# A convolution with a soft mixture of experts: two pieces of x in one DMA issue, with the loads of taps and w1 between the issues

## The chip, the cores and the metric

The kernel runs on one core of a Trainium2 chip. The metric is the device time of one execution in microseconds (us). The engines are named as in the profile: PE (TensorE, the matmuls; PEld its weight loads), DVE (VectorE), ACT (ScalarE), POOL (GpSimd) and SP (SyncE), which computes nothing here and issues all DMAs.

## The reference

There are two steps. The first is a causal convolution along the sequence with seven taps, where the taps of each token and head are the softmax of `weight_gen`. The second is a soft mixture of experts over the 28,672 rows that come out of it: each of 32 slots takes a softmax-weighted mean of all rows, eight experts work on four slots each, and each row takes a softmax-weighted mean of the 32 slots' outputs.

```python
# x: (8, 3584, 192); weight_gen: (8, 3584, 8 heads, 7 taps)
w = np.exp(weight_gen - weight_gen.max(-1, keepdims=True))
w = w / (w.sum(-1, keepdims=True) + 1e-09)
x_unf = x_pad[:, idx, :].reshape(B, S, K, H, group)      # six rows of zeros ahead of x
x = np.einsum('bshk,bskhg->bshg', w, x_unf).reshape(B * S, D)

logits = x @ phi                                          # (28672, 32)
d = np.exp(logits - logits.max(0)); d /= d.sum(0) + 1e-09 # over the rows
slot_input = (d.T @ x).reshape(E, S_per_e, D)
for e in range(E):
    slot_out[e] = np.maximum(slot_input[e] @ w1[e], 0.0) @ w2[e]
c = np.exp(logits - logits.max(1, keepdims=True)); c /= c.sum(1, keepdims=True) + 1e-09
out = c @ slot_out.reshape(n_slots, D)
```

All data are float32.

## The kernel before

The sequence is cut into 1,104 short stretches of 26 tokens each. Four stretches make a group (276 groups), two groups a pair (138 pairs), and four pairs a block (35 blocks, counted by `k`). x comes in pieces: a piece `t` holds four groups, that is two pairs, so there are 69 pieces and block k reads the pieces 2k and 2k+1. The taps come in chunks of eight groups, one chunk per block.

**Convolution as matmuls.** For each group the seven taps of each token are laid out as a band matrix of 32 x 26, and PE multiplies bands with x (`conv`, L230, 32 matmuls per pair). For this x lies block-diagonally in `big`: a piece fills four fields `h = 0..3`, each on its own 32 partitions and with its own DMA (`loadx`, L156), and the rest of the field was zeroed once at the start. `big` has room for five pieces (`NXS`); `place(t)` says where piece t goes, which is t modulo 5, except that piece 0 goes where piece 4 goes. So a piece can be loaded when the piece that had its place before has been read by PE.

**From taps to bands.** A chunk's taps are loaded (`loadw`, L160, three buffers) and then pass through a chain: `tap_top` on DVE (maximum, L171), `tap_sub` on POOL (L175), `tap_exp` on ACT (L179), `tap_sum` on POOL (L188 to L190), `tap_inv` on DVE (reciprocal, L194), `tap_mul` on POOL (L202, into `wide`), `tap_turn` on DVE (L206, from `wide` into one of three bands).

**The rest of a block.** ACT copies the convolved rows out of PSUM (L236). PE turns them (`pt`, L250), and ACT copies that to `cm` (L257). The pairs are handled further in units of eight pairs, two blocks: PE forms the unit's logits (`ls`, L281), DVE their maximum (`mx`, L288; `mq`, L290), PE spreads it over the partitions (`newmax`, L306), DVE takes the result (`nm`, L310), ACT the exponential (`dd`, L318), DVE turns it (`dt`, L327), and PE adds up slot inputs (`acb`, L346), which DVE gathers in `accS` (L354). From block 2 on, in even blocks `ls` of the unit before stands between the second and third pair, and newmax behind the fourth; in odd blocks acb stands between the third and fourth pair.

**What sets the order.** The operations are recorded by `op(engine, cost, reads, writes, function, ..., late=..., due=...)`, with an estimated cost and, for a DMA, `late`, the time that is allowed from its issue to its landing. A planner, `model`, goes through the list four times. PE's and SP's operations keep the order in which they are recorded; those of DVE, ACT and POOL are placed where the planner finds that they can start, those with the least time to spare first. So another cost or `late` of a DMA, or another order of SP's operations, gives DVE, ACT and POOL another order too. Each engine then works through its list in order: an instruction that waits holds up all behind it.

The loads of a block are recorded behind its conv: the taps of chunk k+4, then the pieces 2k+5 and 2k+6 as their places come free, with a part of w1 (24 parts in all) behind some pieces.

After the last pair, the experts' matmuls (`hidden`, `outputs`) and the output rows (`rows`, L818, and `leave`, L825 and L827) follow.

Of the kernel before, what the change touches and what calls it, by code (L numbers as in the profile page):

```python
# [20 lines left out]
SGG = 4  # L21
UP = 8
NSG = NG // SGG
NBC = SGG * 4 * 2
L = 32
CH = 2
NCH = -(-NG // (4 * CH))
# [3 lines left out]
NS, E, SE, F = 32, 8, 4, 1024  # L31
# [5 lines left out]
Q = 4  # L37
TR = 3 * 32 + T
NXS = 5
# [6 lines left out]
def place(t):  # L46
    return t % NXS if t else NXS - 1
# [3 lines left out]
def conv_soft_moe(ctx, tc, xh, wh, phi, w1a, w1b, w2, out):  # L51
# [101 lines left out]
    def loadx(t):  # L153

        for h in range(4):
            SY.dma_start(xbd[32 * h : 32 * h + 32, place(t), h], xh[t, h])  # L156

    def loadw(c):
        n = min(CH, NG // 4 - CH * c)
        SY.dma_start(taps[c % NTAP][:, 0:n], wh[c, :, 0:n])  # L160

    ALL = slice(0, CH)
    tops, tsums = {}, {}

    def each(t, n):
# [249 lines left out]
        SY.dma_start(w2_at(e, 0, FC), w2[:, e])  # L415

    def pace(e, what, src):
        op(PO, 0.15, [what], [("w2", e), x_of(NSG - NXS + e // 2)], mark, e, src)
        op(SP, 0.4, [("w2", e)], [], loadw2, e)

    logit, dispatched = {}, {}
# [7 lines left out]
    def op(eng, cost, reads, writes, f, *a, late=0.0, due=None):  # L429


        i = len(ops)
        preds = {writer[r] for r in (*reads, *writes) if r in writer}
        for r in writes:
            preds |= set(readers.get(r, ()))
            writer[r], readers[r] = i, []
        for r in reads:
            readers.setdefault(r, []).append(i)
        preds.discard(i)
        ops.append((eng, cost, late + 0.1 * (eng == "TE"), preds, due, f, a))  # L440

    def x_of(t):
        return ("x", place(t))

    def conv_reads(p):
        return {x_of(g // SGG) for g in (2 * p, 2 * p + 1)} | {("band", p // 4 % NBAND, p // 2 % CH)}

    def tm_of(p):
        u, pr = unit(p)
# [2 lines left out]
    VE, AC, PO, TE, SP = "VE", "AC", "PO", "TE", "SP"  # L452
    op(SP, 0.65, [], [("w", 0, 0), ("w", 0, 1)], loadw, 0, late=2.6)
    op(SP, 0.65, [], [("w", 1, 0), ("w", 1, 1)], loadw, 1, late=2.6)
    op(SP, 2.6, [], [x_of(0)], loadx, 0, late=2.8)
    op(SP, 0.6, [], [("w", 2, 0), ("w", 2, 1)], loadw, 2, late=3.0)
    op(SP, 1.9, [], [x_of(1)], loadx, 1, late=3.0)
    for t, es in ((2, (PO, AC, AC, AC)), (3, (PO, AC, VE, AC)), (NXS, (PO, PO, AC, AC))):
        for h, e in enumerate(es):
            op(e, 0.77, [], [("z", t, h)], clear, place(t), h, {PO: G, AC: A, VE: V}[e])  # L460
        if t < NXS:
            op(SP, 1.9, [("z", t, h) for h in range(4)], [x_of(t)], loadx, t, late=3.0)
    for i in range(NCV):
        op(AC, 0.47, [], [("cv", i)], clear_cv, i)
    op(VE, 0.3, [], [("tm", u, pr) for u in range(NTM) for pr in range(UP)], edges)
# [79 lines left out]
    for k in range(BLOCKS):  # L545
# [8 lines left out]
        for c in range(3, NCH):  # L554
            if k == max(0, c - 2):
                chain(c)
        for c in range(NTAP, NCH):
            if k == max(0, c - 4):
                op(SP, 0.4, [], [("w", c % NTAP, b) for b in range(CH)], loadw, c, late=4.0)
        for t in range(NSG):  # L560
            if (SGG * t + SGG - 1) // (2 * Q) == k:
                if t + NXS < NSG:
                    for i in (NXS - 1, NXS) if t == 0 else (t + NXS,):
                        op(SP, 2.0, [("z", i, h) for h in range(4)], [x_of(i)], loadx, i, late=3.0)
                    if t == 0:
                        op(SP, 0.45, [], ["phi"], SY.dma_start, phi_sb, phi, late=3.0)
                for j in range(2 * (E + E // 2)):
                    if 2 + 5 * j // 2 == t:
                        e, f = j // 2, slice(F // 2 * (j % 2), F // 2 * (j % 2 + 1))
                        to, w, e = (w1a_sb, w1a, e) if e < E else (w1b_sb, w1b, e - E)  # L570
                        op(SP, 0.4, [], [], SY.dma_start, to[:, e, f], w[:, e, f])
        for p in ps:
            e = p - (PAIRS - 9)
            if e >= 0 and e % 2 == 0:
# [357 lines left out]
```

## Time and profile before

| | us |
|---|---|
| median of three runs | 309.73 (305.82 to 310.65) |
| the profiled execution's own time | 308.94 |
| span in the profile | 307.2 |
| PE busy | 265.4 (86%) |
| DVE busy | 197.8 (64%) |
| ACT busy | 190.3 (62%) |
| POOL busy | 146.5 (48%) |
| convolution's first and last matmul | 8.2 and 222.4 |
| x: issues, one's landing (median) | 276, 3.2 |
| taps: issues, one's landing (median) | 35, 3.7 |
| mean granted clock of PE | 0.945 of full speed |

The profiled execution's own time is 1.74 us longer than its span, which runs from the first to the last instruction. A row of a timeline gives the start and the duration in us, the engine and the line, the operation, what it writes and reads, how many instructions are merged in it, and in brackets the engine's idle time before it with what ended it. Issues on SP's queue are the time in which SP hands a DMA over, not that in which it moves. A row of waits gives the total, the number of times and the longest.

### The profile page before, as it was taken

Reading aid. Unit: us, or ns where it says so; the run is one execution under the profiler, and the core shown is the slowest. Engines: PE = TensorE matmul, PEld = TensorE weight load, DVE = VectorE, ACT = ScalarE, POOL = GpSimd, SP = SyncE. Lnnn points to the kernel's source line nnn. Section 1 sums busy time; section 2 is a strip of 40 time slices with the busy share of each in tenths; the row PEclk is TensorE's granted clock in tenths of the full one; section 3 lists DMA queues with packets and bytes.
Section 4 is the critical chain, followed back from the end, with each engine's and each line's share of the span. In section 5 each row is a group of like instructions: output and inputs, shape, how many; then the busy total and the mean of one; then the engine's idle time right before and its main releaser. Section 6 shows DMA issues by size and latency. Waiting matters only on the chain.

```text
span 307.2 us, 15262 instructions
## 1 busy us (share of the span) xinstructions
PE 265.4 (86%) x6646; PEld 213.6 (70%) x6646; DVE 197.8 (64%) x337; ACT 190.3 (62%) x399; POOL 146.5 (48%) x254
## 2 busy tenths in 40 slices
PE   8898996999998999899899989999999888899100
PEld 8887975889887988789788878898768622233000
DVE  8867738775975957868478568573158489994100
ACT  9886673767685778667566666675422188786300
POOL 8856456654568194774654553520027345540000
PEclk9999998999999999999999999999999999879555
DMA  6758666867675767767567667657647079999994
GB/s 184 217 171 236 201 199 195 208 178 207 197 211 150 225 188 207 207 192 212 168 183 212 189 185 211 189 156 227 217 121 296 2 303 403 399 398 398 399 399 177
DMA packets 30161, 69.24 MB, mean 225 GB/s; under 512 B 6288, under 2 KB 11152, under 8 KB 30096
## 3 DMA queue, kind: packets, MB, share of 16 engines
q1 hardware_dynamic: 30096, 68.28, 69.2%
q8 instruction: 52, 0.85, 1.1%
q14 instruction: 13, 0.11, 0.1%
HBM read 46.21 MB, written 22.04 MB: 222 GB/s over the span
## 4 chain that ended last, share of the span: by engine, by line
PE 73%; DVE 6%; DMA 6%; issue 5%; ACT 2%; POOL 2%; DVEq 0%; POOLq 0%; ACTq 0%
PE cv L230 31%; PE pt L250 15%; PE ls L281 8%; PE acb L346 8%; PE po L818 5%; DMA out<-big 4%; PE so L763 2%; PE hpb L742 2%; PE acb L306 2%; DMA taps<-wh 2%; DVE big L825 1%; ACT big L825 1%; DVE band L206 1%; DVE big L362 1%; DVE cT L404 1%
## 5 line engine op out<-in xcount | busy, mean ns | idle before, releaser
L230 PE MATMUL cv<-big,band 128*26 128x96 f32 x4416 | 112.0, 250 | 4.0 <-issue 2.6
L230 PEld LDWEIGHTS cv<-big,band 128*26 128x26 f32 x4416 | 100.8, 130 | 13.8 <-issue 8.1
L236 ACT COPY tm<-cv 128x384 f32<-128x384 f32 x138 | 66.5, 484 | 62.8 <-PE cv L230 62.5
L206 DVE STREAM_TRANSPOSE band<-wide 128x1664 f32<-128x1664 f32 (+1 forms) x37 | 65.4, 1771 | 6.1 <-POOL wide L202 6.0
L250 PE MATMUL pt<-ident,tm 122*128 122x122 f32 x414 | 51.0, 273 | 0.0
L257 ACT COPY cm<-pt 128x416 f32<-128x416 f32 x103 | 48.1, 512 | 1.7 <-PE pt L250 0.6
L250 PEld LDWEIGHTS pt<-ident,tm 122*128 122x128 f32 x414 | 44.7, 145 | 2.3
L202 POOL TENSOR_TENSOR wide<-exps,sum 128x364 f32<-128x364 f32 (+1 forms) x36 | 28.4, 791 | 24.9 <-DVE sum L194 18.6
L818 PE MATMUL po<-cT,so 32*128 32x442 f32 (+3 forms) x256 | 35.4, 644 | 5.6 <-DVE big L825 3.0
L175 POOL TENSOR_TENSOR taps<-taps,top 128x364 f32<-128x364 f32 (+1 forms) x36 | 28.5, 793 | 18.3 <-DVE top L171 17.9
L825 ACT COPY big<-po 128x884 f32<-128x884 f32 (+2 forms) x33 | 28.5, 894 | 9.3 <-PE po L818 5.3
L188 POOL TENSOR_TENSOR si<-exps 128x208 f32<-128x208 f32 x32 | 20.2, 632 | 28.4 <-ACT exps L179 28.0
L818 PEld LDWEIGHTS po<-cT,so 32*128 32x128 f32 (+1 forms) x256 | 12.3, 172 | 27.5 <-ACT big L825 15.7
L281 PE MATMUL ls<-cm,phi_sb 128*32 128x208 f32 x544 | 29.1, 338 | 2.0 <-issue 1.9
L346 PE MATMUL acb<-tm,dt 128*32 128x193 f32 x544 | 27.4, 328 | 3.3 <-issue 3.3
L288 DVE TENSOR_REDUCE mx<-ls 128x1 f32<-128x416 f32 x17 | 10.0, 588 | 28.1 <-PE ls L281 28.1
L87 POOL TENSOR_TENSOR LT<-LT,rm 128x544 f32<-128x544 f32 (+1 forms) x16 | 17.9, 1119 | 17.0 <-DVE rm L85 17.0
L171 DVE TENSOR_REDUCE top<-taps 128x52 f32<-128x364 f32 (+1 forms) x37 | 17.7, 484 | 12.8 <-DMA taps<-wh 12.0
L281 PEld LDWEIGHTS ls<-cm,phi_sb 128*32 128x32 f32 x544 | 17.8, 109 | 7.9 <-issue 3.6
L346 PEld LDWEIGHTS acb<-tm,dt 128*32 128x32 f32 x544 | 17.8, 110 | 7.4 <-issue 4.7
L99 POOL TENSOR_TENSOR LT<-LT,sm 128x544 f32<-128x544 f32 (+1 forms) x16 | 17.9, 1120 | 6.3 <-DVE sm L97 6.2
L825 DVE COPY big<-po 128x884 f32<-128x884 f32 (+2 forms) x16 | 16.7, 1047 | 6.2 <-ACT big L825 2.2
(113 smaller groups left out, 262.3 us busy)
## 6 DMA issues: line engine op xcount, KB each, us to landing
big<-xh SPq DMA_DIRECT2D x276, 96.0 KB, 3.2
out<-big SPq DMA_DIRECT2D x36, 442.0 KB, 6.9
taps<-wh SPq DMA_DIRECT2D x34, 182.0 KB, 3.7
big<-w SPq DMA_DIRECT2D x8, 768.0 KB, 4.5
out<-big SPq DMA_DIRECT2D x11, 468.0 KB, 4.7
w1a_sb<-w1a SPq DMA_DIRECT2D x16, 256.0 KB, 4.2
w1b_sb<-w1b SPq DMA_DIRECT2D x8, 256.0 KB, 3.6
out<-big SPq DMA_DIRECT2D x2, 234.0 KB, 2.3
```

What stands on the lines that cost most here:

```text
L175: eng.tensor_tensor(out=t, in0=t, in1=each(tops.pop((c, b.start)), b.stop - b.start), op=ALU.subtract)
L188: eng.tensor_tensor(out=s, in0=t[:, :, :, 0:4], in1=t[:, :, :, 4:8], op=ALU.add)
L202: eng.tensor_tensor(out=dst, in0=exps[c % NEX][:, b, :, 0:KT], in1=each(m, n), op=ALU.mult)
L206: V.transpose(bands[c % NBAND][:, b].rearrange("p b j l -> p (b j l)"), wide[:, b].rearrange("p b j -> p (b j)"))
L230: P.matmul(cv[32 * blk : 32 * blk + T, o : o + 4 * GW], bands[g // 8 % NBAND][:, g // 4 % CH, :, i], xbd[:, place(t), :, b * GW : (b + 1) ...
L236: copy(tms[u % NTM][:, pr, 1 : 2 * D + 1], cvs[p % NCV][:, 0 : 2 * D])
L250: P.transpose(pt[:, at, 0:TR], tms[u % NTM][0:TR, pr, 1 + 128 * i : 129 + 128 * i], ident[0:TR, 0:TR])
L257: copy(cms[u].rearrange("p a i b j -> p (a i b) j")[:, at : at + n], pts.pop((k, j)).rearrange("p i (b j) -> p (i b) j", j=32)[:, 0:n, 0:T])
L281: P.matmul(lp[32 * blk : 32 * blk + 32, lo:hi, par, 0:T], phi_sb[:, 2 * par + i, :], cm[:, lo:hi, 1 if i else 2 * par, blk, :], start=(i = ...
L346: P.matmul(ac[32 * q : 32 * q + 32], dt[:, g, :], tm[:, g // 2, o : o + D + 1], start=(g < 4), stop=(g + 4 >= 2 * n))
L818: P.matmul(po[dst : dst + hi - lo, at, 0 : n * T], so[32 * q : 32 * q + 32, lo:hi], cT[32 * q : 32 * q + 32, g0 : g0 + n, 0:T], start=True ...
L825: (V.tensor_copy if done[1] % 3 == 1 else A.copy)(ot.rearrange("p (q c) -> p q c", c=n * T), po[:, 0 : len(qs), 0 : n * T])
```

## The change

Three things change, all in the loads of the convolution.

- `loadxh(t, n, h)` loads field h of n pieces in one DMA. With n = 2 the two places must lie side by side, and each partition gets two runs of 3,072 bytes. In block k the pieces 2k+4 and 2k+5 are loaded, with four such issues; in each fifth block, where the second of the two goes to the first place of `big`, and in block 0, eight issues of one piece are made. The last piece is alone.
- x's dependences are kept by field, `("x", place, h)`, and the planner's figures for a load change: an issue of x costs 0.55 with `late=3.4` (2.0 for four with 3.0 before), one of taps 0.45 with 3.2 (0.4 with 4.0 before).
- In a block from block 1 on, the taps stand behind the first quarter of x's issues and w1's part behind the second, where taps stood first before. In block 0, pieces 4 and 5 stand ahead of the taps of chunks 3 and 4 and of phi.

`HALF` has one entry, all 128 partitions, so taps and w1 are not cut.

```diff
     def loadx(t):
         for h in range(4):
-            SY.dma_start(xbd[32 * h : 32 * h + 32, place(t), h], xh[t, h])
+            loadxh(t, 1, h)
+
+    def loadxh(t, n, h):
+        p = place(t)
+        SY.dma_start(xbd[32 * h : 32 * h + 32, p : p + n, h], xh[t : t + n, h].rearrange("t r c -> r t c"))
...
+    HALF = slice(0, 128),
...
-    def x_of(t):
-        return ("x", place(t))
+    def x_of(t, n=1, hs=range(4)):
+        return [("x", place(i), h) for i in range(t, t + n) for h in hs]
...
-        for c in range(NTAP, NCH):
-            if k == max(0, c - 4):
-                op(SP, 0.4, [], [("w", c % NTAP, b) for b in range(CH)], loadw, c, late=4.0)
-        for t in range(NSG):
-            if (SGG * t + SGG - 1) // (2 * Q) == k:
-                if t + NXS < NSG:
-                    for i in (NXS - 1, NXS) if t == 0 else (t + NXS,):
-                        op(SP, 2.0, [("z", i, h) for h in range(4)], [x_of(i)], loadx, i, late=3.0)
-                    if t == 0:
-                        op(SP, 0.45, [], ["phi"], SY.dma_start, phi_sb, phi, late=3.0)
-                for j in range(2 * (E + E // 2)):
-                    if 2 + 5 * j // 2 == t:
...
+        cs = [c for c in range(NTAP, NCH) if k == max(0, c - 4)]
+        parts = [(SP, 0.45, [], [("w", c % NTAP, i)], loadw, c, r) for c in cs for i, r in enumerate(HALF)]
+        w1 = [(SP, 0.45, [], [], loadw1, j, r) for j in range(2 * (E + E // 2)) if (2 + 5 * j // 2) // 2 == k
+              for r in HALF]
+        xs = []
+        for t in (2 * k, 2 * k + 1):
+            if t == 0:
+                xs += [(i, 1, h) for i in (NXS - 1, NXS) for h in range(4)]
+            elif t % 2 == 0 and t + NXS - 1 < NSG:
+                n = min(2, NSG - (t + NXS - 1))
+                if n == 2 and place(t + NXS) == 0:
+                    xs += [(i, 1, h) for i in (t + NXS - 1, t + NXS) for h in range(4)]
+                else:
+                    xs += [(t + NXS - 1, n, h) for h in range(4)]
+        if k == 0:
+            rest_of, parts, w1 = [*parts, (SP, 0.45, [], ["phi"], lambda: SY.dma_start(phi_sb, phi)), *w1], [], []
+        else:
+            rest_of = []
+        for m, (t, n, h) in enumerate(xs):
+            op(SP, 0.55, [("z", t, h)], x_of(t, n, (h,)), loadxh, t, n, h, late=3.4)
+            if (m + 1) % (len(xs) // 4) == 0:
+                for l in (parts, w1) if m * 4 // len(xs) % 2 == 0 else (w1, parts):
+                    if l:
+                        o = l.pop(0)
+                        op(*o, late=3.2 if o[4] is loadw else 0.0)
+                        break
+        for o in (*rest_of, *parts, *w1):
+            op(*o, late=3.2)
```

More of the change, by code (lines that the diff above doesn't have):

```diff
@@ L155, in loadx, with loadw, loadw1 @@
         for h in range(4):
-            SY.dma_start(xbd[32 * h : 32 * h + 32, place(t), h], xh[t, h])
-    def loadw(c):
-        n = min(CH, NG // 4 - CH * c)
-        SY.dma_start(taps[c % NTAP][:, 0:n], wh[c, :, 0:n])
+            loadxh(t, 1, h)
+    def loadxh(t, n, h):
+        p = place(t)
+        SY.dma_start(xbd[32 * h : 32 * h + 32, p : p + n, h], xh[t : t + n, h].rearrange("t r c -> r t c"))
+    def loadw(c, r=slice(0, 128)):
+        n = min(CH, NG // 4 - CH * c)
+        SY.dma_start(taps[c % NTAP][r, 0:n], wh[c, r, 0:n])
+    def loadw1(j, r):
+        e, f = j // 2, slice(F // 2 * (j % 2), F // 2 * (j % 2 + 1))
+        to, w, e = (w1a_sb, w1a, e) if e < E else (w1b_sb, w1b, e - E)
+        SY.dma_start(to[r, e, f], w[r, e, f])
     ALL = slice(0, CH)
+    HALF = slice(0, 128),
     tops, tsums = {}, {}
@@ L417, in pace @@
     def pace(e, what, src):
-        op(PO, 0.15, [what], [("w2", e), x_of(NSG - NXS + e // 2)], mark, e, src)
+        op(PO, 0.15, [what], [("w2", e), *x_of(NSG - NXS + e // 2)], mark, e, src)
         op(SP, 0.4, [("w2", e)], [], loadw2, e)
@@ L440, in op @@
         ops.append((eng, cost, late + 0.1 * (eng == "TE"), preds, due, f, a))
-    def x_of(t):
-        return ("x", place(t))
+    def x_of(t, n=1, hs=range(4)):
+        return [("x", place(i), h) for i in range(t, t + n) for h in hs]
     def conv_reads(p):
-        return {x_of(g // SGG) for g in (2 * p, 2 * p + 1)} | {("band", p // 4 % NBAND, p // 2 % CH)}
+        return {x for g in (2 * p, 2 * p + 1) for x in x_of(g // SGG)} | {("band", p // 4 % NBAND, p // 2 % CH)}
     def tm_of(p):
@@ L454, in conv_soft_moe @@
     op(SP, 0.65, [], [("w", 1, 0), ("w", 1, 1)], loadw, 1, late=2.6)
-    op(SP, 2.6, [], [x_of(0)], loadx, 0, late=2.8)
+    op(SP, 2.6, [], x_of(0), loadx, 0, late=2.8)
     op(SP, 0.6, [], [("w", 2, 0), ("w", 2, 1)], loadw, 2, late=3.0)
-    op(SP, 1.9, [], [x_of(1)], loadx, 1, late=3.0)
+    op(SP, 1.9, [], x_of(1), loadx, 1, late=3.0)
     for t, es in ((2, (PO, AC, AC, AC)), (3, (PO, AC, VE, AC)), (NXS, (PO, PO, AC, AC))):
@@ L461, in conv_soft_moe @@
         if t < NXS:
-            op(SP, 1.9, [("z", t, h) for h in range(4)], [x_of(t)], loadx, t, late=3.0)
+            op(SP, 1.9, [("z", t, h) for h in range(4)], x_of(t), loadx, t, late=3.0)
     for i in range(NCV):
```

3 lines of the change are left out of this document (removed).

## The prediction, made before the changed kernel was run

> **What bounds the kernel now.** I read the page first, for the busy shares and the chain of waits that ended last.
>
> ```profile
> PE 265.4 (86%) x6646; PEld 213.6 (70%) x6646; DVE 197.8 (64%) x337; ACT 190.3 (62%) x399; POOL 146.5 (48%) x254
> PE 73%; DVE 6%; DMA 6%; issue 5%; ACT 2%; POOL 2%; DVEq 0%; POOLq 0%; ACTq 0%
> ```
>
> TensorE is busy 86% of the span and holds 73% of the chain. The change takes no matmul away, so it can give back only time in which PE waits, and it touches only the loads of the first 222 us. So I looked there for PE's gaps. "Issue" in the chain is time in which PE waited for nothing that the profile shows; no load can be charged with it, and I leave it. One gap stands out in PE's timeline, and DVE's timeline shows what ended it:
>
> ```profile
> 45.91 1.63 PE L230 MATMUL cv<-big,band 128*26 128x96 f32 x64
> 50.31 0.36 PE L306 MATMUL acb<-mq,sel 128*128 128x5 f32 x2 [2.77 <-DVE mq L290]
> 52.42 3.27 PE L230 MATMUL cv<-big,band 128*26 128x96 f32 x96
> ```
>
> ```profile
> 47.08 0.53 DVE L171 TENSOR_REDUCE top<-taps 128x52 f32<-128x364 f32 x1 [3.67 <-DMA taps<-wh]
> 47.53 1.90 DVE L206 STREAM_TRANSPOSE band<-wide 128x1664 f32<-128x1664 f32 x1
> 49.36 0.55 DVE L288 TENSOR_REDUCE mx<-ls 128x1 f32<-128x416 f32 x1
> 49.94 0.22 DVE L290 TENSOR_SCALAR mq<-ls,mx 128x4 f32<-128x4 f32 x1
> ```
>
> PE stood still for 2.77 us before newmax (L306), which needs mq. DVE works its list in order, and mx and mq stood behind the reduction top of chunk 9 (by the order), which waited 3.67 us for its taps, though PE was in block 6 and reads band 9 only in block 9. PE waited for a load that it did not need yet.
>
> The gap had a second price. In a table by stretch (columns: stretch, sum, busy time and count of PE, PEld, DVE, ACT, POOL, then the granted clock, DMA share, GB/s):
>
> ```profile
> 48.00:50.30 2.30, 0.00 (x0) 0.02 (x1) 2.27 (x4) 1.26 (x3) 2.06 (x5) 1.00 0.43 109
> 50.30:52.40 2.10, 2.09 (x14) 1.81 (x14) 1.95 (x6) 1.41 (x3) 1.94 (x6) 0.74 0.77 241
> 52.40:54.00 1.60, 1.60 (x41) 1.58 (x44) 1.60 (x2) 0.01 (x1) 0.71 (x1) 0.50 0.83 241
> 54.00:56.00 2.00, 2.00 (x76) 1.88 (x72) 1.48 (x3) 1.19 (x3) 0.37 (x1) 0.82 0.87 195
> 128.00:132.00 4.00, 2.85 (x85) 2.25 (x76) 2.71 (x5) 1.73 (x5) 2.19 (x4) 1.00 0.76 224
> ```
>
> After the gap the granted clock fell to 0.74, 0.50 and 0.82. Lost: 2.10 x 0.26 + 1.60 x 0.50 + 2.00 x 0.18 = 1.7 us. In the last row a gap of 4.00 - 2.85 = 1.15 us left the clock at 1.00. [...]
>
> Why were the taps late? The issues on SP's queue just before:
>
> ```profile
> 36.37 0.38 SPq L160 DMA_DIRECT2D taps<-wh  x1
> 36.84 4.97 SPq L156 DMA_DIRECT2D big<-xh  x8
> 41.86 0.42 SPq L686 DMA_DIRECT2D w1a_sb<-w1a  x1
> 42.38 0.38 SPq L160 DMA_DIRECT2D taps<-wh  x1
> 42.85 4.71 SPq L156 DMA_DIRECT2D big<-xh  x8
> 47.66 1.48 SPq L160 DMA_DIRECT2D taps<-wh  x1
> ```
>
> From 36.37 to 47.66, 11.29 us, issues fill 0.38 + 4.97 + 0.42 + 0.38 + 4.71 = 10.86 us: SP is full here, and taps leave when their turn comes; those that DVE waits for until 47.08 left at 42.38. A block is 11.29 / 2 = 5.6 us. All issues of x together:
>
> ```profile
> L156 SPq DMA_DIRECT2D big<-xh x276: 310/419/1851, 1.8 to 206.8; - x138
> DMA to landing us min/median/max: 2.0/3.2/5.0
> ```
>
> An issue of x takes 0.42 us of SP (min, median, max in ns), and its data lands after 3.2 us. The line of the taps' issues says of theirs:
>
> ```profile
> DMA to landing us min/median/max: 2.4/3.7/5.8
> ```
>
> **Part 1: two pieces in one issue.** x falls from 276 issues to 100 of two runs and 76 of one, so 176; per block of four pairs from 8 x + taps + w1 (10 issues) to 4 + 1 + 1 = 6, and 10 in each fifth block, where the two places don't lie side by side. SP's load per block falls from 5.4 us (10.86 / 2) to about 6 x 0.42 = 2.5 us if two runs cost what one does, and 4 x 0.84 + 0.8 = 4.2 us if they cost twice that. No row shows such an issue. A taps issue has 128 rows and took 0.38, so rows are not what costs; I take 0.42 and keep 0.84 for the range. Either way SP has room, the backlog is gone within a few blocks, and the wait at 47 us goes: -2.77 - 1.7 = -4.5 us. What is late next there is mx itself, which then follows the end of ls.
>
> **Part 2: what is issued first.** On SP's queue at the start, before (L160 taps, L156 x, L686 phi and w1):
>
> ```order
> L156 DMA big_67<-xh 32x768 x12
> L160 DMA taps0_84<-wh 128x364
> L160 DMA taps1_85<-wh 128x364
> L156 DMA big_67<-xh 32x768 x8
> L686 DMA phi_sb_62<-phi 128x128
> L156 DMA big_67<-xh 32x768 x4
> L160 DMA taps2_86<-wh 128x364
> ```
>
> And now (L164 taps, L160 x, L582 phi, L169 w1):
>
> ```order
> L160 DMA big_67<-xh 32x768 x20
> L164 DMA taps0_84<-wh 128x364
> L164 DMA taps1_85<-wh 128x364
> L582 DMA phi_sb_62<-phi 128x128
> L160 DMA big_67<-xh 32x2x768
> L164 DMA taps2_86<-wh 128x364
> L160 DMA big_67<-xh 32x2x768
> L169 DMA w1a_sb_63<-w1a 128x512
> L160 DMA big_67<-xh 32x2x768 x3
> ```
>
> Taps 3 and 4 move behind the eight issues of pieces 4 and 5. Their times before:
>
> ```profile
> 9.58 1.25 SPq L160 DMA_DIRECT2D taps<-wh  x2
> 10.93 4.37 SPq L156 DMA_DIRECT2D big<-xh  x8
> 15.35 1.44 SPq L686 DMA_DIRECT2D phi_sb<-phi  x1
> ```
>
> Taps 3 leaves not at 9.58 but at about 9.8 + 4.37 = 14.2, 4.6 us later, and lands near 17.9 instead of 13.3 (3.7 us each). phi has the same ten issues ahead of it in another order; it stays near 15.3 and costs nothing while it lands before the first ls.
>
> The kernel's planner knows of this and has rebuilt DVE's list. Chunk 3's work on DVE, before (sum3 and band0 are chunk 3's; mx0, mq, nm0 belong to unit 0's maximum):
>
> ```order
> L171 TENSOR_REDUCE top3_0_387<-taps0_84 128x52
> L171 TENSOR_REDUCE top4_0_390<-taps1_85 128x52
> L206 STREAM_TRANSPOSE band2_92<-wide_89 128x1664
> L194 RECIPROCAL sum3_0_453<-sum3_0_453 128x52
> L288 TENSOR_REDUCE mx0_525<-ls_99 128x1
> L290 TENSOR_SCALAR mq_131<-ls_99,mx0_525 128x4
> L206 STREAM_TRANSPOSE band0_90<-wide_89 128x1664
> L310 TENSOR_REDUCE nm0_577<-acb_100 128x1
> ```
>
> And now:
>
> ```order
> L216 STREAM_TRANSPOSE band2_92<-wide_89 128x1664
> L181 TENSOR_REDUCE top3_0_465<-taps0_84 128x52
> L181 TENSOR_REDUCE top4_0_470<-taps1_85 128x52
> L181 TENSOR_REDUCE top5_0_495<-taps2_86 128x52
> L298 TENSOR_REDUCE mx0_514<-ls_99 128x1
> L300 TENSOR_SCALAR mq_131<-ls_99,mx0_514 128x4
> L320 TENSOR_REDUCE nm0_550<-acb_100 128x1
> L204 RECIPROCAL sum3_0_518<-sum3_0_518 128x52
> L216 STREAM_TRANSPOSE band0_90<-wide_89 128x1664
> ```
>
> The reciprocal of sum3 and band 3 went from ahead of nm0 to behind it. nm0 needs PE's newmax, and block 3's conv needs band 3. The durations on that path, from PE, DVE and GpSimd:
>
> ```profile
> 19.13 1.60 PE L281 MATMUL ls<-cm,phi_sb 128*32 128x208 f32 x32
> 22.38 0.39 PE L306 MATMUL acb<-mq,sel 128*128 128x4 f32 x2
> 22.62 1.45 PE L250 MATMUL pt<-ident,tm 122*128 122x122 f32 x12
> 24.00 2.21 PE L230 MATMUL cv<-big,band 128*26 128x96 f32 x96
> ```
>
> ```profile
> 19.21 0.48 DVE L194 RECIPROCAL sum<-sum 128x52 f32<-128x52 f32 x1 [1.53 <-POOL sum L190]
> 21.55 1.90 DVE L206 STREAM_TRANSPOSE band<-wide 128x1664 f32<-128x1664 f32 x1
> 23.38 0.12 DVE L310 TENSOR_REDUCE nm<-acb 128x1 f32<-128x4 f32 x1
> ```
>
> ```profile
> 19.77 0.83 POOL L202 TENSOR_TENSOR wide<-exps,sum 128x364 f32<-128x364 f32 x1 [0.59 <-DVE sum L194]
> ```
>
> Now newmax ends at 22.38 + 0.39 = 22.8, nm 22.9, reciprocal 23.4, the product on GpSimd (0.08 later, as 19.77 stands behind 19.21 + 0.48) 24.3, the turn 26.2. PE is through with pt at 24.0: a new gap of 2.2 us. Bounds: 0 if chunk 3 had other cover (I see none: all four steps stand in order), and 3 us if the load comes later still. The clock may fall behind this gap as it did behind 2.77 us: between 0 and 1.7 us; 2.2 lies nearer to 2.77 than to 1.15, but is shorter than the one case seen, so I take 1.0. [...]
>
> **Part 3: x is asked for later.** A two-run issue waits until both its places are free, so piece 2k+4 leaves one piece later than before. The time it has left, from block 27 to block 29:
>
> ```profile
> 176.46 2.21 PE L230 MATMUL cv<-big,band 128*26 128x96 f32 x96
> 189.15 2.04 PE L230 MATMUL cv<-big,band 128*26 128x96 f32 x88
> ```
>
> Piece 54 is read at 176.46 + 2/3 x 2.21 = 177.9, piece 58 is wanted at 189.15: 11.2 us. The last of the four issues starts 3 x 0.42 + 0.38 + 0.42 = 2.1 us after the first and lands by 2.1 + 3.2 = 5.3. Cover enough, so nothing. At the far end (0.84 per issue, one of the long issues as at 47.66, 1.1 us more, landing at 5.0) it is 4.4 + 5.0 = 9.4, still inside. Taps now stand behind the wait for that piece too; what covers that is the three blocks, 16.8 us, from a chunk's top to its use.
>
> **Sum.** The profiled execution took 308.94 us: 308.94 - 4.5 + 2.2 + 1.0 = 307.7, so 308. The median of the runs, 309.73, is 0.8 above the profiled one; the runs lie from 305.82 to 310.65, a spread as large as the gap and its clock together, so I add nothing for it.
>
> **Rivals.**
> - No new gap at 24 us, only the old one gone: 308.94 - 4.5 = 304.5. For it: SP is less loaded. Against: the four steps behind newmax. 0.10.
> - The old gap stays, since SP's issue time was not what held the taps, and the new one comes: 308.94 + 2.2 + 1.0 = 312.1. For it: the landing, 3.2 to 5.8 us, is much longer than an issue. Against: SP full for 10.86 of 11.29 us. 0.12. [...]
> - Slower: DVE meets taps that have not landed, in front of mx. What the planner allows from the taps' issue to their landing falls from 0.4 + 4.0 = 4.4 to 0.45 + 3.2 = 3.65 us, against a measured median of 3.7 and a longest of 5.8, and by the order top stands directly ahead of mx in 9 of 17 units, in 4 before. Before, taps held DVE eight times:
>
> ```profile
> DVE top L171 <- DMA taps<-wh: 12.0, 8, 3.7
> ```
>
> and only one of the eight reached PE. Each that does costs 2.77 + 1.7 = 4.5 us: 312 with one, 316.7 with two, which is slower by over 2%. It decides once a wait outlasts the ls that runs before mx. One 0.08, two or more 0.05.
> - Slower by x: if landings double with the bytes, 4.4 + 6.4 = 10.8, and a taps issue that holds SP 0.4 us for its buffer passes 11.2. One us lost per two blocks, in 12 such pairs, is 320. 0.05.
>
> **Chances.** Forecast 0.60. The range takes in the forecast's own 306.7 to 309 and the first two rivals with one wait of the third: 304.5 to 313. A measurement here tells about 2% from no change, so 303.5 and 315.9 are the lines. Faster 0.04 (scatter below the first rival), slower 0.10, within 0.86.
>
> **What would show it.** Right: no wait of DVE on taps near 47 us and a PE gap of about 2.2 us before block 3's conv, ended by band; fewer back-to-back issues on SP from 27 us on. Wrong: PE waits for x at the starts of blocks; several waits of mq on PE later on; an issue of two runs that takes 0.8 us; landings of x over 6 us.

## The result: slower by 4.4%, against a forecast of no change

The changed kernel takes 320.56 us in the median of its runs (318.24 to 330.13), the kernel before 307.77 us in runs on the same chip (304.77 to 310.65). The ratio is 1.044, 95% interval 1.030 to 1.058; like all ratios below it is taken over each kernel's fast runs alone, so it can differ a little from the quotient of the medians. The prediction said 308.0, with 304.5 to 313.0 as its range.

The profiled execution of the changed kernel took 318.24 us (span 316.5), that of the kernel before 308.94 (span 307.2), so 9.3 us are to be found. The medians lie 12.8 us apart; the traces tell of the 9.3 us between these two executions alone. From the page of the kernel after, the busy shares, the DMA queues (packets, MB, share of 16 engines), the chain, and the two rows of the convolution (count, busy us, mean ns, then idle time and what ended it):

```profile
PE 265.5 (84%) x6646; PEld 213.8 (68%) x6646; DVE 198.8 (63%) x337; ACT 188.5 (60%) x399; POOL 146.0 (46%) x254
...
q1 hardware_dynamic: 28496, 68.27, 75.7%
q8 instruction: 52, 0.85, 1.2%
...
PE 69%; DMA 7%; issue 7%; DVE 5%; ACT 3%; POOL 2%; SPq 1%; POOLq 0%; ACTq 0%; DVEq 0%
...
L240 PE MATMUL cv<-big,band 128*26 128x96 f32 x4416 | 114.3, 249 | 12.8 <-issue 9.3
L240 PEld LDWEIGHTS cv<-big,band 128*26 128x26 f32 x4416 | 101.9, 130 | 23.5 <-issue 16.4
```

The rows of the page of before that answer to them and were not shown yet:

```profile
q1 hardware_dynamic: 30096, 68.28, 69.2%
...
L230 PE MATMUL cv<-big,band 128*26 128x96 f32 x4416 | 112.0, 250 | 4.0 <-issue 2.6
L230 PEld LDWEIGHTS cv<-big,band 128*26 128x26 f32 x4416 | 100.8, 130 | 13.8 <-issue 8.1
```

PE does the same work (265.4 and 265.5 us) and stands still for longer, mostly for "issue", which is time in which it waits for nothing that the profile shows. The transfers carry the same 68.3 MB, but their packets now occupy 75.7% of the DMA engines' span and not 69.2%, in a longer span. (The idle time of PEld, the weight loads, overlaps PE's own and is not added to it.) The waits of PE by what ended them (us in total, times, longest), first after, then before:

```profile
PE cv L240 <- issue: 9.3, 14, 1.8
PE acb L356 <- issue: 4.3, 3, 2.2
PE cv L240 <- DVE band L216: 3.2, 2, 2.2
...
PE ls L291 <- DMA phi_sb<-phi: 2.3, 1, 2.3
```

```profile
PE acb L346 <- issue: 3.3, 4, 1.1
PE acb L306 <- DVE mq L290: 3.2, 2, 2.8
...
PE cv L230 <- issue: 2.6, 6, 0.7
...
PE ls L281 <- issue: 1.9, 3, 1.1
PE cv L230 <- DVE band L206: 1.0, 1, 1.0
```

Between the convolution's first and last matmul, I summed all of PE's gaps over 0.12 us by what ended them. Issue went from 8.2 to 15.1 us (+6.9), phi from 0 to 2.3, band from 1.0 to 3.2 (+2.2), mq from 2.8 to 0, ACT from 0 to 0.2: together +8.8 of the 9.3. The time that the clock took is the same in both, 1.7 us, though in another place.

**What the prediction named at the start.** PE's timeline of the kernel after has both gaps:

```profile
21.57 1.61 PE L291 MATMUL ls<-cm,phi_sb 128*32 128x208 f32 x32 [2.27 <-DMA phi_sb<-phi]
22.97 1.53 PE L240 MATMUL cv<-big,band 128*26 128x96 f32 x64
24.43 0.39 PE L316 MATMUL acb<-mq,sel 128*128 128x4 f32 x2
24.68 1.45 PE L260 MATMUL pt<-ident,tm 122*128 122x122 f32 x12
28.30 1.88 PE L240 MATMUL cv<-big,band 128*26 128x96 f32 x80 [2.18 <-DVE band L216]
```

The second is the one forecast: DVE's timeline shows nm, the reciprocal and the turn of band 3 behind newmax, in the order that the prediction read.

```profile
24.86 0.16 DVE L320 TENSOR_REDUCE nm<-acb 128x1 f32<-128x4 f32 x1 [0.77 <-PE acb L316]
24.93 0.47 DVE L204 RECIPROCAL sum<-sum 128x52 f32<-128x52 f32 x1
26.34 1.91 DVE L216 STREAM_TRANSPOSE band<-wide 128x1664 f32<-128x1664 f32 x1 [0.93 <-POOL wide L212]
```

The first was not forecast. The issues on SP's queue ahead of phi:

```profile
8.70 5.99 SPq L160 DMA_DIRECT2D big<-xh  x10
14.74 2.35 SPq L164 DMA_DIRECT2D taps<-wh  x2
17.14 0.42 SPq L582 DMA_DIRECT2D phi_sb<-phi  x1
```

phi left at 17.14 and not near 15.3, because the two issues of taps took 2.35 us here (1.25 before) and the pieces of x took some 0.8 us longer; its landing ended at 21.4. The lists of DMA issues have its time to landing (KB, then us), after and before:

```profile
phi_sb<-phi SPq DMA_DIRECT2D x1, 64.0 KB, 4.3
```

```profile
phi_sb<-phi SPq DMA_DIRECT2D x1, 64.0 KB, 3.0
```

**What the prediction expected at 47 us** came out: in DVE's timeline, top no longer waits for taps, and mx waits for ls alone.

```profile
46.12 0.53 DVE L181 TENSOR_REDUCE top<-taps 128x52 f32<-128x364 f32 x1
50.40 0.59 DVE L298 TENSOR_REDUCE mx<-ls 128x1 f32<-128x416 f32 x1 [3.74 <-PE ls L291]
```

**What it left out** is "issue". The longest such gap in PE's timeline:

```profile
170.25 0.50 PE L356 MATMUL acb<-tm,dt 128*32 128x193 f32 x7
172.97 2.13 PE L356 MATMUL acb<-tm,dt 128*32 128x193 f32 x25 [2.22 <-issue]
```

PE stops in the middle of 32 matmuls whose inputs are all there. The table by stretch around it (as in the prediction: stretch, sum, PE, PEld, DVE, ACT, POOL, granted clock, DMA share, GB/s; shares a little over 1 are packets that overlap in the records, up to 22 at a time):

```profile
168.50:170.70 2.20, 2.20 (x103) 1.87 (x92) 2.20 (x3) 1.36 (x4) 0.20 (x1) 1.00 1.06 214
170.75:172.95 2.20, 0.00 (x1) 0.00 (x0) 2.20 (x3) 0.83 (x3) 1.39 (x2) 1.00 0.99 227
173.00:175.00 2.00, 2.00 (x35) 1.47 (x39) 0.27 (x1) 0.00 (x0) 0.00 (x0) 0.59 0.55 159
175.00:177.00 2.00, 2.00 (x35) 1.71 (x28) 0.86 (x2) 0.48 (x1) 0.82 (x1) 0.56 0.02 3
```

The DMA engines are full ahead of the gap and in it. Behind it the granted clock falls to 0.59 and 0.56 in these stretches: the 1.7 us that the end of the gap at 47 us had saved are lost here.

### The profile page after: what moved, and what is told of

Same layout as the page of the kernel before. It is cut to its first block, busy times and chain, and to the rows that moved or that the text cites. A ratio compares the mean times of both kernels' runs of the same rounds, so it can differ in the third digit from the quotient of the medians.

```text
span 316.5 us, 15079 instructions
## 1 busy us (share of the span) xinstructions
PE 265.5 (84%) x6646; PEld 213.8 (68%) x6646; DVE 198.8 (63%) x337; ACT 188.5 (60%) x399; POOL 146.0 (46%) x254
## 2 busy tenths in 40 slices
DMA packets 28560, 69.22 MB, mean 219 GB/s; under 512 B 4688, under 2 KB 9552, under 8 KB 28496
## 3 DMA queue, kind: packets, MB, share of 16 engines
q1 hardware_dynamic: 28496, 68.27, 75.7%
## 4 chain that ended last, share of the span: by engine, by line
PE 69%; DMA 7%; issue 7%; DVE 5%; ACT 3%; POOL 2%; SPq 1%; POOLq 0%; ACTq 0%; DVEq 0%
PE cv L240 31%; PE pt L260 14%; PE ls L291 8%; PE acb L356 8%; DMA out<-big 5%; PE po L841 3%; PE so L786 2%; PE hpb L765 2%; PE acb L316 2%; ACT big L848 2%; DMA phi_sb<-phi 1%; DVE big L848 1%; DVE big L372 1%; DVE cT L414 1%; DMA big<-xh 1%
## 5 line engine op out<-in xcount | busy, mean ns | idle before, releaser
L240 PE MATMUL cv<-big,band 128*26 128x96 f32 x4416 | 114.3, 249 | 12.8 <-issue 9.3
L240 PEld LDWEIGHTS cv<-big,band 128*26 128x26 f32 x4416 | 101.9, 130 | 23.5 <-issue 16.4
L356 PE MATMUL acb<-tm,dt 128*32 128x193 f32 x544 | 28.4, 334 | 4.3 <-issue 4.3
L291 PE MATMUL ls<-cm,phi_sb 128*32 128x208 f32 x544 | 28.2, 339 | 2.7 <-DMA phi_sb<-phi 2.3
L181 DVE TENSOR_REDUCE top<-taps 128x52 f32<-128x364 f32 (+1 forms) x37 | 17.6, 483 | 12.9 <-DMA taps<-wh 12.2
L356 PEld LDWEIGHTS acb<-tm,dt 128*32 128x32 f32 x544 | 19.0, 111 | 8.0 <-issue 5.5
```

Of the source, the lines that this page charges most:

```text
L240: P.matmul(cv[32 * blk : 32 * blk + T, o : o + 4 * GW], bands[g // 8 % NBAND][:, g // 4 % CH, :, i], xbd[:, place(t), :, b * GW : (b + 1) ...
L291: P.matmul(lp[32 * blk : 32 * blk + 32, lo:hi, par, 0:T], phi_sb[:, 2 * par + i, :], cm[:, lo:hi, 1 if i else 2 * par, blk, :], start=(i = ...
L356: P.matmul(ac[32 * q : 32 * q + 32], dt[:, g, :], tm[:, g // 2, o : o + D + 1], start=(g < 4), stop=(g + 4 >= 2 * n))
```

## What PE waits for: its own instructions

The page lists 52 packets of kind "instruction" on queue 8, 0.85 MB, so 16 KB each. PE executes 13,292 instructions (6,646 matmuls and as many weight loads); that is 256 per packet, one packet per 128 matmuls. The trace has each packet's start and length, and I set them beside PE's issue gaps. All issue gaps over 0.5 us of the kernel after, with the instruction packet that ended last before PE went on, the time from its end to PE's restart, the busy share of the 16 DMA engines (queue 1) in the 3 us ahead of that packet's start, and the number of matmuls done, modulo 128:

```
gap              us    packet           restart after its end   DMA busy before it   matmuls mod 128
 43.47- 45.28   1.81    42.70- 43.98    1.30                    1.01                 83
 62.90- 64.05   1.15    61.23- 62.55    1.49                    1.03                 77
 77.52- 78.50   0.98    75.90- 77.16    1.34                    1.06                 74
 95.10- 95.91   0.81    93.28- 94.42    1.48                    0.84                 69
100.88-101.51   0.63    98.63- 99.92    1.59                    1.02                 67
131.79-133.62   1.83   130.86-132.26    1.36                    1.04                 59
170.75-172.97   2.22   170.16-171.52    1.45                    0.94                 49
187.42-189.21   1.79   186.44-187.63    1.58                    0.83                 44
207.41-208.03   0.62   205.40-206.55    1.48                    0.77                 39
```

PE goes on 1.3 to 1.6 us after the packet, every time. In the 13 profiles of this case (before, after and the eleven experiments below) there are 97 issue gaps over 0.5 us in the convolution's stretch, and all 97 end 1.2 to 1.7 us after the end of an instruction packet; the 83 shorter ones do so too. Of PE's 63 gaps that something else ended, 7 do, and a moment picked at random does so in 9 to 12 cases of 100.

The last column tells where in the program the gaps lie. From the first row to the last it falls by 83 - 39 = 44. In the same time the trace has 88 instructions of PE's sequencer (waits for semaphores), which take up as much of the program as 44 matmuls with their weight loads. In all 13 profiles the two agree to half a matmul. So the gaps lie at the borders of blocks of 256 instructions, and since all 97 end behind an instruction packet, I read them as waits for instructions. Not every border has one: of the 46 packets in this stretch of the kernel after, 37 are followed by no gap over 0.5 us.

The packets ahead of a gap start late by PE's own progress. In the kernel after, PE has done 155 matmuls on average, beyond 128 for each packet before it, when such a packet starts, and 110 when one of the other 37 does; the mean is higher ahead of gaps in each of the 13 profiles. They hardly take longer once they have started (1.27 and 1.17 us). When PE asked for a packet is not recorded.

What goes with a late start is in the sixth column: 0.95 on average ahead of the nine packets above, 0.74 ahead of the others in the same stretch (in the kernel before 0.76 for its six and 0.68 for 40). Most borders show no gap over 0.5 us (37 of 46), but what the issue gaps add up to is not small: 8.2 us of 308.94 before and 15.1 of 318.24 after.

How often the DMA engines are full, in one table for all kernels: stretches of 1 us, from 20 us to the last matmul of the convolution, in which queue 1 keeps them busy for 95% or more, beside the sums of PE's gaps in the profiled execution and the times of all runs.

```
kernel                                  full DMA, us   issue gaps   other gaps   clock loss   median us   ratio to before [95%]
before                                       5            8.2          3.8          1.7        307.8
after                                       80           15.1          5.6          1.7        320.6      1.044 [1.030, 1.058]
after, one run per issue                    11            8.4          6.5          5.1        312.3      1.019 [1.008, 1.029]
after, start as before                      84           21.9          4.0          5.1        324.7      1.057 [1.045, 1.068]
after, half the bytes                        6            3.1          3.5          0          298.5      0.977 [0.967, 0.987]
after, two waves                            52           14.8          4.3          1.7        315.7      1.030 [1.022, 1.039]
after, paced                                40           10.7          5.4          1.7        314.7      1.016 [1.006, 1.026]
after, fields 0 2 1 3                       67           12.4          5.8          3.4        315.9      1.024 [1.017, 1.031]
after, one run, start as before             12           10.5          5.3          0          312.0      1.009 [1.001, 1.017]
the same, fields 0 2 1 3                     5            4.8          5.5          0          308.6      1.011 [1.002, 1.020]
after, paced, start as before, 0 2 1 3      41           14.7          3.8          1.7        (307.9 to 315.3)
before, fields 0 2 1 3                       9            4.7          6.9          1.7        310.6      1.003 [0.994, 1.012]
before, fields 0 2 1 3, planner's costs      9            4.3          3.6          0          304.1      0.991 [0.986, 0.996]
```

The sums close: the time from the convolution's first to its last matmul, less gaps and clock loss, lies between 199.3 and 201.8 us in all of them but the one with half the bytes (196.7). What the kernels that load all of x differ by are, but for 2.5 us, the gaps and the clock. Issue gaps rise with the time of full engines on the whole, but not in step: two waves have 52 us and 14.8, paced 40 and 10.7, and one run per issue 11 to 12 us with 8.4 or 10.5.

Each kernel's gaps come from one execution, and executions of one kernel differ by some us, so a step of 3 us in one column is a hint and not a measurement; the ratios are.

## The experiments

**One run per issue.** Every issue of two runs becomes two of one run, at the same place in the lists and behind the same waits; PE, DVE, ACT and POOL have the lists of the changed kernel.

```diff
-        p = place(t)
-        SY.dma_start(xbd[32 * h : 32 * h + 32, p : p + n, h], xh[t : t + n, h].rearrange("t r c -> r t c"))
+        for i in range(t, t + n):
+            SY.dma_start(xbd[32 * h : 32 * h + 32, place(i), h], xh[i, h])
```

> As the changed kernel, but each issue of two runs is made as two issues of one run in a row; the lists of PE, DVE, ACT and POOL are the same. The changed kernel lost time in PE gaps that the profile calls issue (9.3 us before cv, 2.6 in the kernel before), at phi (2.3 us) and at band 3 (2.2 us). Theory F: PE's own program is fetched by DMA (the queue of kind instruction, 52 packets), and the fetch stands behind the bytes of x that are in flight; with one run per issue eight issues in flight are 768 KB instead of 1,536. Then issue before cv falls to 3 to 5 us and the time to 310 to 314 us. Theory G: it is the gating, all of two pieces at once in mid-block, whatever the issues: issue stays at 8 to 10 and the time at 317 to 321. Theory O: it is the new order of DVE, ACT and POOL: unchanged too, 317 to 320.

312.33 us (309.37 to 313.85), ratio 1.0185 [1.0083, 1.0287]. From its page, the DMA queue and the convolution's row:

```profile
q1 hardware_dynamic: 30096, 68.28, 70.4%
...
L240 PE MATMUL cv<-big,band 128*26 128x96 f32 x4416 | 114.8, 253 | 6.4 <-issue 3.2
```

The time is inside what was expected. Issue gaps are back at 8.4 us with the new order and the new waits for x still in place, so neither of those made them: they came with the two runs in one issue. The new gap of band stays (3.2 us with the old 1.0), phi's falls to 0.7. Gaps for mq come back with SP slow again, 2.7 us in all, the longest, 1.97 us, from 112 to 114 us behind a top that waited 3.6 us for its taps. About 60% of the loss, 0.026 of 0.044, goes with the two runs; the intervals leave wide room around that share.

**Block 0 in the old order.** The changed kernel, but taps 3 and 4 are issued ahead of pieces 4 and 5, and phi right behind them. The planner makes new lists for DVE, ACT and POOL.

```diff
...
-            rest_of, parts, w1 = [*parts, (SP, 0.45, [], ["phi"], lambda: SY.dma_start(phi_sb, phi)), *w1], [], []
+            for o in parts:
+                op(*o, late=3.2)
+            parts = []
...
         for m, (t, n, h) in enumerate(xs):
...
+            if k == 0 and m == len(xs) - 1:
+                op(SP, 0.45, [], ["phi"], lambda: SY.dma_start(phi_sb, phi), late=3.2)
```

> As the changed kernel, but in block 0 the taps of chunks 3 and 4 stand ahead of pieces 4 and 5 again, and phi directly behind them, as before. Mine: the waits for phi (2.3 us) and for band 3 (2.2 us) go and nothing takes their place, so 4.4 us less than the changed kernel, 313 to 316 us, with the issue gaps as large as they were. Rival: those two waits only took up time that is lost later anyway (x or taps not there), and the time stays at 317 to 320.

324.68 us (321.42 to 330.96), ratio 1.0565 [1.0447, 1.0682]: a miss. PE's waits:

```profile
PE cv L240 <- issue: 13.9, 14, 2.3
PE acb L356 <- issue: 5.0, 3, 2.9
```

The gaps at the start did go (band is back at 1.0 us and there is no wait for phi). In this execution they came back, and more, as issue gaps: 21.9 us. So the 4.4 us at the start were not saved. That the kernel is slower than the changed one is not shown, since the two intervals overlap; that it is 4.4 us faster, as expected, is ruled out by them.

**Half the bytes.** Each issue of two runs moves the first half of its columns; half of the columns of those pieces of x are never loaded. The lists are the same. (The expectation's "two thirds" is too much: 9.8 MB fewer are moved, 36% of x.)

```diff
-        SY.dma_start(xbd[32 * h : 32 * h + 32, p : p + n, h], xh[t : t + n, h].rearrange("t r c -> r t c"))
+        w = NBC * GW // n
+        SY.dma_start(xbd[32 * h : 32 * h + 32, p : p + n, h, 0:w], xh[t : t + n, h, :, 0:w].rearrange("t r c -> r t c"))
```

> As the changed kernel with the same issues and the same lists on all engines, but each issue of two runs moves only the first half of each run (1,536 bytes instead of 3,072), so two thirds of x's later columns keep old data. Theories F and G (bytes of a burst hold up the fetch of PE's program): issue before cv falls from 9.3 to 2 to 4 us, and the time by 6 to 8 us to 310 to 313. Theory O (order of the engines): unchanged, 316 to 320.

298.52 us (296.20 to 300.34), ratio 0.9766 [0.9665, 0.9867], far lower than expected. Of the 22.0 us between the two profiled executions, issue gaps are 12.0, other gaps 2.2 and the clock 1.7; 5.1 us of the convolution's stretch lie in no gap, and what made them is open. From its page:

```profile
q1 hardware_dynamic: 28496, 58.44, 61.4%
...
L241 PE MATMUL cv<-big,band 128*26 128x96 f32 x4416 | 109.0, 248 | 7.1 <-issue 3.1
```

The packets are as many as in the changed kernel (28,496) and the issues too, with the same two runs; only the bytes are fewer. So it is neither the number of packets nor the form of the issue by itself that makes the issue gaps. With 6 us of full engines instead of 80, issue gaps fall to 3.1 us, under those of the kernel before. The time does not tell what the fetches alone are worth, since fewer bytes saved time elsewhere too.

**Two waves.** The four two-run issues of a block are split, two pieces apart: fields 0 and 1 with one pair of pieces, fields 2 and 3 with the next, so that half as much of x is issued at a time. The planner makes new lists. The heart of the edit:

```diff
...
+            for h in range(4):
+                i = 2 * k + NXS - 1 + h // 2
+                if i + 1 < NSG and place(i + 1) != 0:
+                    xs.append((i, 2, h))
...
```

> As the changed kernel with issues of two runs, but in two waves: fields 0 and 1 of the pieces 2k+4 and 2k+5 when piece 2k is read, fields 2 and 3 of the pieces 2k+5 and 2k+6 when piece 2k+1 is read. The count of issues stays, the burst is half as large and comes twice as often. Theory G (the burst): issue before cv falls to 4 to 6 us, time 312 to 315. Theory F (bytes in flight) the same or a little less. Theory O: 316 to 321.

315.66 us (314.32 to 316.69), ratio 1.0303 [1.0219, 1.0387], just above what was expected. PE's waits put 10.3 us to issue at the convolution alone:

```profile
PE cv L240 <- issue: 10.3, 13, 1.9
```

Issue gaps are 14.8 us: halving the bursts did little to them, though the DMA engines were full for 52 us and not 80. The ratio's interval overlaps with that of the changed kernel, so a gain is not shown. This run speaks against a simple rule by which full engines alone set the gaps.

**Paced.** The changed kernel, with a transfer of 4 bytes that nothing waits for behind every issue of two runs. The two runs stay; SP makes two issues for each 192 KB, at 0.42 us each an estimated half of the pace.

```diff
+        if n == 2:
+            i = pads.pop()
+            SY.dma_start(scratch[0:1, i : i + 1], phi[0:1, 0, 0:1])
```

> The changed kernel with a transfer of 4 bytes, which nothing waits for, issued on SP behind every issue of two runs. PE, DVE, ACT and GpSimd have the same lists; SP issues x at about half the pace (two issues of 0.42 us per 192 KB), and the tiny transfers take up half the places of what is in flight. Theory P (x's bytes, handed over twice as fast, stand in the DMA engines ahead of PE's own instruction fetches, and PE runs dry at the borders of its 16 KB instruction blocks): PE's gaps put down to issue fall from 15.1 us to about 8 (8.35 with one run per issue), landings of x from 4.9 us to about 4, and the time to 310 to 314. Rival R (it is the form of the transfer, two runs per partition row, that is slow in the engines, whatever the pace): issue gaps stay at 13 to 16 us and the time at 317 to 321. Rival S (SP gets too slow again): the wait of top for taps at 47 us comes back with a gap of about 2.7 us before newmax, and the time is 313 to 316 with issue gaps of 8.

314.65 us (311.21 to 316.23), ratio 1.0161 [1.0063, 1.0258]. The convolution's row of its page:

```profile
L245 PE MATMUL cv<-big,band 128*26 128x96 f32 x4416 | 113.1, 250 | 13.6 <-issue 9.4
```

The ratio is near that of one run per issue (1.0185), with the two runs in place and 100 more DMAs: more work for SP made the kernel faster, since the ratio's interval lies wholly below that of the changed kernel (1.030 to 1.058). So the form of the transfer is not what costs most. Theory R, which had 317 to 321 us, is out. Theory P's numbers were a little too good: issue gaps fell to 10.7 us and not to 8. The gap at 47 us that theory S feared did not come, but two others for mq did, of about 1 us each at 22 and 112 us; the gap for phi went. The 4-byte transfers may also take places among what is in flight, which in the traces of the kernels before and after is at most 8 DMAs of SP at a time; so whether the pace counts or the bytes in flight was not told apart. Landings of x can't be read from this trace.

**The fields of x in another order.** The fields are issued 0, 2, 1, 3, first in the changed kernel and then in the kernel before; the lists of the other engines are the same.

```diff
-        p = place(t)
-        SY.dma_start(xbd[32 * h : 32 * h + 32, p : p + n, h], xh[t : t + n, h].rearrange("t r c -> r t c"))
+        p, f = place(t), (0, 2, 1, 3)[h]
+        SY.dma_start(xbd[32 * f : 32 * f + 32, p : p + n, f], xh[t : t + n, f].rearrange("t r c -> r t c"))
```

> The changed kernel with the four fields of x (32 partitions each) issued in the order 0, 2, 1, 3 in place of 0, 1, 2, 3; all else is the same, and so are the lists of the other engines. If two neighbouring fields hold each other up on the way into the memory (theory Q), landings of x fall from 4.9 us towards 4, issue gaps from 15.1 to 8 to 12 us, and the time to 311 to 315. If the backlog is of bytes alone (theory P), nothing changes: landings 4.7 to 5.1, issue gaps 13.5 to 16.5, 317 to 321.

```diff
-        for h in range(4):
+        for h in (0, 2, 1, 3):
```

> The kernel before, with the four fields of x issued in the order 0, 2, 1, 3. Theory Q: landings of x fall from 3.2 us to under 2.9, issue gaps from 8.2 to 4 to 6 us, the time to 303 to 306. Theory P: as the kernel before, 306 to 310, issue gaps 7.5 to 9, landings 3.2, and the gap before newmax at 47 us stays.

The changed kernel: 315.90 us (314.24 to 317.64), ratio 1.0239 [1.0165, 1.0313], between the two expectations; the median landing of two runs fell from 4.9 to 4.4 us, issue gaps from 15.1 to 12.4. Its interval overlaps a little with that of the changed kernel, so a small gain is suggested and not shown. The kernel before: 310.59 us (307.05 to 317.07), ratio 1.0028 [0.9935, 1.0121], no difference. Issue gaps fell there too, as theory Q had it (8.2 to 4.7 us), but mq's waits grew, by the view of PE's waits, from 3.2 us to

```profile
PE acb L306 <- DVE mq L290: 6.0, 4, 3.4
```

and took the gain back in this execution. In the kernel before the share of full DMA time did not fall (5 and 9 us), so by what the order would help there stays open.

**One run per issue, with block 0 in the old order**, and then the same with the fields 0, 2, 1, 3. The edits are those above, put together.

> The changed kernel with both earlier edits: block 0 keeps the order of the kernel before (taps 3 and 4 ahead of pieces 4 and 5, phi right behind them), and every issue of two runs is two of one run. The gaps at the start (phi 0.67, band 2.17 us in the kernel with one run alone) should go. If edits add up, the time is that of one run alone, 312.3, less 2.8: 309 to 310, with issue gaps of 8 to 9 us. Rival: what is saved at the start comes back later as issue gaps, as in the kernel with the start alone (21.9 for 15.1): issue gaps 11 to 14 us, 312 to 316.

> The changed kernel with all three edits: one run per issue, block 0's order of the kernel before, and the fields of x in the order 0, 2, 1, 3. If the order of the fields helps with every form of issue (issue gaps fell from 8.2 to 4.7 us in the kernel before, from 15.1 to 12.4 in the changed one), issue gaps fall from 10.5 us to about 7 and the time from 312.0 to 308 to 309.5, level with the kernel before. If that was the scatter of single runs, issue gaps stay at 9.5 to 11.5 us and the time at 311 to 313.

312.04 us (309.76 to 315.92), ratio 1.0089 [1.0005, 1.0172], and 308.64 us (304.23 to 311.14), ratio 1.0108 [1.0015, 1.0201], each against the kernel before in its own comparison. In the first, issue gaps rose to 10.5 us from the 8.4 of one run per issue alone, so a part of the start's saving seems to have come back, as far as one execution tells; its time lies at the lower end of the rival's range. In the second they fell to 4.8 us in the profile and the median is where it was expected, but the two ratios agree within their intervals, so from these two nothing can be said for the order of the fields.

**The planner told what the trace measured.** The kernel before, with the fields 0, 2, 1, 3, and SP's costs as measured: 2.4 us for a piece of x (4.71 to 4.97 us for two) and 4.7 us to the landing of taps. That is the time from the issue at 42.38 to top's start at 47.08 and lies between the median of 3.7 and the longest of 5.8. The idea is that the gap at 47 us came of a list made for a faster SP.

```diff
-                op(SP, 0.4, [], [("w", c % NTAP, b) for b in range(CH)], loadw, c, late=4.0)
+                op(SP, 0.4, [], [("w", c % NTAP, b) for b in range(CH)], loadw, c, late=4.7)
...
-                        op(SP, 2.0, [("z", i, h) for h in range(4)], [x_of(i)], loadx, i, late=3.0)
+                        op(SP, 2.4, [("z", i, h) for h in range(4)], [x_of(i)], loadx, i, late=3.0)
```

> The kernel before with the fields in the order 0, 2, 1, 3 and with SP's costs in the planner set to what the trace measured: 2.4 us for a piece of x in place of 2.0, and 4.7 us to the landing of taps in place of 4.0; the planner then makes new lists for DVE, ACT and GpSimd. If the gap before newmax at 47 us (2.8 us, 3.4 with the other order of the fields) comes only from the planner's taking SP to be faster than it is, the waits of mq fall from 5.6 us to under 1, the clock loss of 1.7 us goes, and with issue gaps of 5 to 7 us the time is 302 to 305. Rival: other waits take their place in the new lists (tops, bands), and the time is 306 to 311.

304.05 us (302.53 to 309.02, ten runs), ratio 0.9912 [0.9862, 0.9963]: faster than the kernel before by 0.9%, which is clear of its interval though small, and faster than the changed kernel. The mq gaps and the time came as the first expectation had them; issue gaps, at 4.3 us, came below it. In DVE's timeline mx and mq now come first and top behind them:

```profile
45.10 0.55 DVE L288 TENSOR_REDUCE mx<-ls 128x1 f32<-128x416 f32 x1
45.69 0.22 DVE L290 TENSOR_SCALAR mq<-ls,mx 128x4 f32<-128x4 f32 x1
...
46.95 0.47 DVE L171 TENSOR_REDUCE top<-taps 128x52 f32<-128x364 f32 x1
```

mq's waits on PE fell to 0.9 us in all and no clock was lost. The same order of fields with the old table kept the gap (the 6.0 us above), so new figures in the planner's table are enough to remove it. How much of the 0.9% is theirs and how much the fields' is not told apart by times: the interval of the kernel before with the fields alone, 0.994 to 1.012, touches this one.

**All three edits on two runs per issue**: paced, block 0 in the old order, fields 0, 2, 1, 3.

> The changed kernel, still with two runs per issue, with a transfer of 4 bytes behind each such issue, block 0's order of the kernel before, and the fields in the order 0, 2, 1, 3. If pace, field order and start add up: issue gaps of 10.7 us less about 3 = 7 to 8.5, start gaps of 4.4 us down to 1 to 1.5, the time 313 to 314 less 5: 307 to 310. If the saving at the start comes back as issue gaps (as it did without the pacing, 21.9 us for 15.1): 312 to 318.

Inconclusive. One run took 307.91 us and three took 315.00 to 315.30, among them the profiled one, whose issue gaps are 14.7 us. No ratio is given; what divides its runs is open.

## Why the prediction was wrong

- **The gap at 47 us**: right. SP has room, top does not wait, and mq's 2.77 us are gone. DVE still waits for taps as much as before (12.2 us in all, eleven times), and, as the forecast had it, none of it reaches PE through mq.
- **The clock's 1.7 us there**: right that they go with the gap; but as much is lost behind the issue gap of 2.22 us at 173 us, so nothing was saved.
- **An issue of two runs takes 0.42 us**: right. The two kinds together have a median of 422 ns in the row below, and the 100 issues of two runs alone 425.
- **The new gap at band 3**: right, 2.18 us against 2.2.
- **The clock behind it, 1.0**: 0 in this execution, behind 2.18 and behind 2.27 us. The 306.7 in the prediction's account of its range is its 307.7 less this 1.0.
- **phi "costs nothing"**: mis-sized by 2.3 us. Before, it had only some 0.8 us of cover: it left at 15.35, landed 3.0 later and was read at 19.13. The same issues stood ahead of it after, but it left 1.8 us later and its landing took 1.3 us more.
- **x is asked for later, "nothing"**: right in what it cost, not in the landing. In the line of x's issues of the kernel after, the time to landing has a median of 4.6 us and a maximum of 7.6 (3.2 and 5.0 before), and still only a few waits of PE are put to x:

```profile
L160 SPq DMA_DIRECT2D big<-xh x176: 310/422/1612, 1.8 to 216.6; - x176
...
  PEld cv L240: 0.9, 6
...
DMA to landing us min/median/max: 2.0/4.6/7.6
```

- **The step that failed** stands under "What bounds the kernel now": of "issue", "no load can be charged with it, and I leave it". "Issue" was 5% of the chain before and 8.2 us of gaps, and the loads could be charged with it: I read them as PE's waits for its own instructions, and they grow and shrink with how x is handed over (15.1 us with two runs per issue, 8.4 with one). That term, set to nothing, measured +6.9 us. With phi it makes 9.2 us, as much as the whole difference between the two profiled executions; the other terms, -2.8 for mq, +2.2 for band and 0 for the clock, nearly cancel.
- **The rivals.** The one priced at 320 by longer landings of x had one thing right, since the median landing of two runs grew by half, and the wrong path: x itself came in time. That its price is near the result is luck. Landings over 6 us, one of the signs of being wrong, were seen.

What is shown: that the gaps lie at the borders of instruction blocks and end with instruction packets that start late; that issue gaps and time rise with two runs per issue (8.4 to 15.1 us of issue gaps, 312.3 to 320.6 us), and fall when only the pace (10.7 and 314.7 us) or only the bytes (3.1 and 298.5 us) are cut. What is argued: that the packets start late because they queue behind x inside the DMA engines. The trace has the engines fuller ahead of late packets, but not the queue itself, and two waves does not fit a simple form of it.

## What to carry to other kernels

Time of PE that waits for nothing the profile shows is not beyond the reach of the loads: set its gaps beside the packets of kind "instruction", and count the fetches of PE's own program (here, where it is written out without a loop, 16 KB per 128 matmuls, one packet every 4.6 us before and 4.9 us after) as a reader whose data may come late when loads come in bursts (8.2 us of issue gaps before, 15.1 after). Fewer, larger issues relieved SP here, but they also filled the DMA engines in bursts that SP's pace had kept apart (80 us of full engines for 5), and that cost more than it gave (a ratio of 1.044). When a planner orders the work, measured costs in its table can be worth more than another order of transfers.

## What the runs showed of the hardware that I had not expected

- One core's loads at a mean of 66% of the DMA engines' time (from 20 us to the end of the convolution) already went with 8.2 us of issue gaps on PE; with the same bytes in bursts it was 76% and 15.1 us.
- An issue of two runs, 192 KB, costs SP 0.42 us, as one of 96 KB did in the kernel before, so it hands over bytes twice as fast, and the median landing rises only by half (3.2 to 4.9 us).
- The clock behind a gap, in the 13 profiles: with 12 of the 17 gaps of PE of 1.95 to 3.38 us in the convolution the granted clock fell to 0.5 for 3.41 us, which costs 1.7 us; the fall came between 0.7 us ahead of the gap's end and 1.7 us behind it. With the other 5, the longest of 2.94 us, it did not. Of 26 gaps between 1.3 and 1.94 us one had a fall behind it, with a second gap 0.5 us behind the first. So between 2 and 3 us the length of a gap does not settle it: in the kernel after the clock fell behind 2.22 us and not behind 2.27 us. What else it depends on is not shown.
